# Another order for the first block of a fused state-space convolution and gated MLP: which pieces of two spectra PE takes first, and which engine evicts three of them

## The chip, the cores and the metric

One core of one Trainium2 chip. The metric is device time in microseconds of one execution, as the median of the runs; a profile is one more execution, taken by the hardware profiler, whose span runs from the first to the last instruction of the program. Engines are named as in the profile: PE (TensorE matmul) and PEld (its weight loads), DVE (VectorE), ACT (ScalarE), POOL (GpSimd), SP (SyncE, which here only issues transfers).

## The reference

Inputs are bf16: q, k, v of 2048 x 640, a convolution kernel ssm_k of 640 x 2048, and MLP weights of 640 x 1728, twice, and 1728 x 640. Cut to what is computed:

```
k_shift = sum over 4 taps of shifted k * shift_k
kv = k_shift * v
y  = irfft(rfft(kv, 4096) * rfft(ssm_k, 4096))[:2048] + kv * ssm_D
h  = q + layernorm(q) * y          # per channel, along the sequence
n  = layernorm(h)
out = h + (silu(n @ w_gate) * (n @ w_up)) @ w_down
```

## The kernel before

The sequence is cut into four blocks of 512 rows. For block j the kernel builds a spectrum G of its piece of ssm_k ("g") and a spectrum X of its kv, both as matmuls against a cosine and sine basis (WF, in two halves that are loaded apart: planes 0 and 2 use the first, planes 1 and 3 the second). It multiplies spectra on DVE (`mac`), comes back with an inverse transform (`inverse`, L698, basis WI), makes h and its normalised transpose, and runs the MLP (`ffn`, L769 and L845). The MLP of block j is woven into the transforms of block j + 1.

In block 0 every 640-wide row is treated as two halves of 320 columns, so that DVE can begin early. There are four planes (c0 to c3) and two halves: eight pieces for each spectrum.

- An X0 piece (L336 to L342): an even pair of 128x320 matmuls (rows 0 and 2), an eviction of the PSUM tile with a factor 2 (L319 on ACT, L322 on DVE), an odd pair (rows 1 and 3) that accumulates on the same tile and so must wait for that eviction, and a second eviction.
- A G0 piece (L350 to L355): four matmuls, an eviction, two matmuls with the weights "minus" (DVE makes these from WF, L912), an eviction. G0 needs block 0's g transposed: four sets of five transposes on PE (L411), each copied out by L413 on ACT or DVE.
- Block 1's g goes another way: ACT regroups it in one copy (L419), then four DMA transposes (L404, arena<-arena, one for each row r0 to r3) put it in place. Block 1's k comes in through four DMA transposes as well (L404, kT<-in_A_k_dram); these overwrite kT and so wait for the copy of its last column into the halo (L517, ACT). G1's pairs are two 128x320 matmuls, one for each half, with one eviction of 128x640.

There are four PSUM tiles "ps"; a tile is free again when its last eviction is done. Larger buffers lie in an arena of 22 units, given out in the order in which they came free.

`Plan.add` records every operation with its engine, its reads and writes. `Plan.run` then issues them in the order of a table written out by hand, ORDER; this sets the order on each engine, since each engine runs its own instructions in the order of issue and waits for what they depend on:

```
for i in ORDER:
    op = self.ops[max(i, ~i)]
    if i < 0:
        op.fn = op.other[2]
```

A negative entry ~n takes operation n's other engine: DVE in place of ACT for an eviction. Numbers that the change moves and that matter below: 92 to 115 are X0's matmuls and evictions (92/93 and 94/95 for c2's first half, 105 to 108 for c1's second half); 43 to 74 are G0's; 34 to 41 the transposes of block 0's g and their copies; 12, 13, 14, 15 the loads of g, WF's first half, WF's second half and ssm_D; 187 to 190 block 1's k transposes; 194 to 197 block 1's g transposes; 198 to 217 G1; 6 nine matmuls on the identity that PE runs while it waits; 75 and 80 block 0's taps (L490), 221 block 1's.

Of the kernel before, what the change touches and what calls it, by code (L numbers as in the profile page):

```python
# [44 lines left out]
UNITS = 22  # L45
SLOTS = {"row": 5, "sg": 3, "ps": 4, "sm": 10}
ORDER = (
# [943 lines left out]
```

## Time and profile before

| | us |
|---|---|
| median of 3 runs | 252.25 |
| the runs | 251.06, 252.25, 252.71 |
| the profiled execution | 251.19 |
| its span | 249.5 |
| PE busy | 237.7 |
| DVE busy | 197.6 |
| ACT busy | 174.0 |

How to read the rows: in a timeline, the first number is the start in microseconds from the span's start, the second the duration (of the whole group where "xN" stands at the end), then engine, line, operation, tiles written and read, shapes. "[1.03 <-DMA ...]" is the engine's idle time just before and what ended it; "issue" means that nothing that the profile shows was waited for. SPq is SP's instruction that issues a transfer. In rows that end in "KB, 5.8" or "x1, 5.8" the last number is the time from issue to landing.

### The profile page before, as it was taken

The page shows a single profiled execution, that of the slowest core. Times are in us where ns is not written, and L with a number is a line of the kernel's source. Part 1 is how long each engine was busy: PE and PEld are TensorE (multiplying, and loading weights), DVE is VectorE, ACT ScalarE, POOL GpSimd, SP SyncE. Part 2 cuts the span into 40 slices and gives each one's busy share as a digit, 9 for nine tenths or more (in the row PEclk, how much of TensorE's full clock was granted, in tenths as well). Part 3 has the DMA queues.
Part 4 walks back from the last instruction along what each step waited for, and adds up shares of the span by engine and source line. Part 5 has one row for each costly group of instructions (what it writes and reads, how often), then busy time and mean ns, then how long its engine had stood idle before and what let it go on. Part 6 is the DMA issues. An engine that isn't in the chain of part 4 may idle for free.

```text
span 249.5 us, 5148 instructions
## 1 busy us (share of the span) xinstructions
PE 237.7 (95%) x2125; PEld 152.5 (61%) x2125; DVE 197.6 (79%) x250; ACT 174.0 (70%) x300; POOL 52.4 (21%) x53
## 2 busy tenths in 40 slices
PE   3899988999999999999999999999999999999994
PEld 3467655888857766544466676454456785464662
DVE  2779998999999999999999899999999542131222
ACT  2399998999999977969598699984532865325100
POOL 0002002531230313124400503353702110000030
PEclk9999999999999999999999999999999999999999
DMA  6999899287998566690725569789592200000052
GB/s 204 353 264 144 229 342 355 65 208 114 143 297 283 167 99 130 109 206 6 119 43 133 105 94 216 132 155 162 97 206 29 26 0 3 0 0 3 0 79 79
DMA packets 37283, 33.66 MB, mean 135 GB/s; under 512 B 22470, under 2 KB 32076, under 8 KB 37260
## 3 DMA queue, kind: packets, MB, share of 16 engines
q1 hardware_dynamic: 32028, 22.03, 34.0%
q0 software_dynamic: 5232, 11.31, 25.4%
q8 instruction: 16, 0.26, 0.4%
q14 instruction: 7, 0.06, 0.1%
HBM read 16.29 MB, written 4.59 MB: 84 GB/s over the span
## 4 chain that ended last, share of the span: by engine, by line
PE 75%; ACT 9%; DMA 6%; DVE 6%; issue 2%; SPq 1%; DVEq 0%; ACTq 0%
PE ps L769 36%; PE ps L845 23%; PE ps L329 7%; PE ps L698 5%; ACT arena L319 4%; DMA arena<-in_A_ssm_k_dram 4%; DMA arena<-arena 3%; PE ps L490 2%; DVE arena L542 2%; PE ps L833 1%; PE ps L411 1%; ACT arena L419 1%; DVE tT L787 1%; ACT sg L783 1%; ACT row L722 1%
## 5 line engine op out<-in xcount | busy, mean ns | idle before, releaser
L769 PE MATMUL ps<-arena,wgu 128*128 128x512 bf16 (+1 forms) x680 | 118.2, 329 | 0.4 <-ACT arena L413 0.2
L769 PEld LDWEIGHTS <-wgu 128*128 128x128 bf16 x680 | 66.2, 98 | 45.0 <-issue 1.1
L845 PE MATMUL ps<-wd,tT 128*128 128x320 bf16 x416 | 59.1, 299 | 0.0
L845 PEld LDWEIGHTS <-tT 128*128 128x128 bf16 x416 | 39.8, 98 | 17.2 <-issue 1.6
L542 DVE TENSOR_TENSOR arena<-arena 128x2560 bf16<-128x2560 bf16 x30 | 43.9, 1486 | 0.2
L783 ACT ACTIVATE sg<-ps 128x1024 bf16<-128x1024 f32 (+1 forms) x28 | 27.1, 971 | 22.2 <-PE ps L769 22.0
L329 PE MATMUL ps<-arena,WF 128*128 128x320 bf16 x176 | 29.8, 299 | 1.7 <-ACT arena L319 0.9
L785 ACT CAST sg<-ps 128x1024 bf16<-128x1024 f32 (+1 forms) x24 | 23.6, 982 | 8.5 <-PE ps L769 3.6
L610 POOL TENSOR_TENSOR sm<-sm,neghalf 128x4 f32<-128x4 f32 (+1 forms) x10 | 17.9, 1793 | 42.9 <-DVE sm L646 42.6
L243 POOL DMA_DIRECT2D arena<-arena x11 | 13.4, 1218 | 60.7 <-DVE arena L542 27.6
L319 ACT CAST arena<-ps 128x640 bf16<-128x640 f32 (+1 forms) x47 | 24.8, 594 | 1.3 <-PE ps L329 1.0
L787 DVE TENSOR_TENSOR tT<-sg,sg 128x1024 bf16<-128x1024 bf16 (+1 forms) x24 | 15.9, 664 | 11.0 <-ACT sg L785 11.0
L329 PEld LDWEIGHTS <-WF 128*128 128x128 bf16 x176 | 17.1, 97 | 11.1 <-issue 2.7
L545 DVE TENSOR_TENSOR arena<-arena 128x2560 bf16<-128x2560 bf16 x14 | 20.8, 1488 | 0.2
L606 ACT ACTIVATE junk<-arena 128x640 bf16<-128x640 bf16 x28 | 20.6, 745 | 0.4 <-DVE arena L709 0.4
L319 ACT ACTIVATE arena<-ps 128x640 bf16<-128x640 f32 (+1 forms) x32 | 19.8, 654 | 0.8 <-PE ps L329 0.8
L698 PE MATMUL ps<-arena,WI 128*128 128x320 bf16 x96 | 15.8, 299 | 1.0 <-issue 0.8
L709 DVE SCALAR_TENSOR_TENSOR arena<-arena,sm,ps 128x640 bf16<-128x640 bf16 x16 | 13.7, 877 | 3.2 <-ACT ps L707 3.1
L850 ACT ACTIVATE row<-ps,sm 128x640 bf16<-128x640 f32 x12 | 9.5, 791 | 8.6 <-PE ps L845 8.1
L852 POOL DMA_DIRECT2D out_dram<-row x12 | 11.7, 1151 | 14.6 <-ACT row L850 14.6
L707 ACT ACTIVATE ps<-ps,sm 128x640 f32<-128x640 f32 x16 | 11.9, 767 | 3.4 <-PE ps L698 3.3
L698 PEld LDWEIGHTS <-WI 128*128 128x128 bf16 x96 | 9.0, 97 | 5.6 <-issue 1.8
(91 smaller groups left out, 236.8 us busy)
## 6 DMA issues: line engine op xcount, KB each, us to landing
arena<-arena POOLq DMA_DIRECT2D x11, 640.0 KB, 6.2
arena<-in_A_v_dram SPq DMA_DIRECT2D x4, 640.0 KB, 5.1
arena<-in_A_q_dram SPq DMA_DIRECT2D x4, 640.0 KB, 4.5
out_dram<-row POOLq DMA_DIRECT2D x13, 160.0 KB, 4.2
arena<-in_A_ssm_k_dram SPq DMA_DIRECT2D x3, 640.0 KB, 8.8
wd<-in_B_w_down_dram SPq DMA_DIRECT2D x2, 800.0 KB, 7.1
out_dram<-arena POOLq DMA_DIRECT2D x2, 640.0 KB, 5.9
wgu<-in_B_w_gate_dram SPq DMA_DIRECT2D x1, 800.0 KB, 5.9
```

The lines of the kernel that those rows point to most:

```text
L319: (lambda: nc.scalar.activation(dst(), src(), ACT.Copy, scale=2.0)) if twice else (lambda: nc.scalar.copy(dst(), src())),
L329: nc.tensor.matmul(ap(ps)[:, h, 0:NH], w, ap(src)[:, r, h * NH:(h + 1) * NH], start=(first and i == 0), stop=(last and i == len(rs) - 1), ...
L542: dve(1402, lambda: v.tensor_mul(to(), X.part(xs), H.part(hs)), [X.at(xs), H.at(hs)], [at])
L545: added(1402 * n - 69 * (n - 1), lambda: v.tensor_add(to(), to(), b()), to, b, [what], at, n)
L606: act(725, lambda r=r: nc.scalar.activation(waste(), ap(x)[:, r, :], ACT.Square, scale=D ** -0.5, accum_out=sm(s, MSQ, (r,))), [(x, r)], [ ...
L610: nc.gpsimd.tensor_tensor(sm(s, RSTD, rs), sm(s, VAR, rs), ap(neghalf)[:, 0:len(rs)], op=ALU.pow)
L698: nc.tensor.matmul(ap(ps)[:, w, 0:NH], m, src[:, w * NH:(w + 1) * NH], start=(i == 0), stop=(i == len(terms) - 1))
L769: nc.tensor.matmul(split(ap(ps), n)[:, i, :], w(k), ap(hT)[:, k, lo:lo + n], start=(k == 0), stop=(k == KT - 1))
L783: act(905 if wide_ else 490, lambda: nc.scalar.activation(of(sg), of(*gate), ACT.Silu), [(gate[0], gate[1] + i) for i in range(m)] + (psu ...
L785: op = plan.add("act", 905 if wide_ else 490, lambda: nc.scalar.copy(of(co), of(*up)), psu + [sg], [co] + tt, ("dve", 1135 if wide_ else 6 ...
L787: op.rest = dve(602 if wide_ else 336, lambda: nc.vector.tensor_mul(to(), of(sg), of(co)), [sg, co], tt)
L845: nc.tensor.matmul(ap(ps[hf])[:, hf, 0:NH], ap(tT)[:, c * BLK + at:c * BLK + at + P], ap(wd)[:, c, hf * NH:(hf + 1) * NH], start=False, st ...
```

## The change

The first 160 entries of ORDER hold the same operations in another order; from the 161st on the table is the same. Three X0 evictions (93, 95 and 108) go from ACT to DVE, one G0 eviction (54) goes from DVE to ACT; of the four copies of block 0's transposed g, DVE has 35 and 37 in place of 37, 39 and 41. WF's second half (14) is issued before block 0's g (12).

```
--- before.py
+++ after.py
@@ -45,13 +45,13 @@
 ORDER = (
     0, 1, 2, 3, 16, 18, -20, 5, 4, 8, 17, 26, 13, 186, 9, 20, 22, 7, 10, 11, -22, 24, -26, 23, 75, 76, 77, 78, 79,
-    6, 193, 80, 81, 82, 30, 92, 93, 15, 12, 38, 83, 34, -40, 14, 36, 32, 35, 94, 27, -38, 95, 96, 97, 42, 28, 40,
...
+    0, 1, 2, 3, 16, 18, -20, 5, 4, 8, 17, 26, 13, 186, 9, 20, 22, 7, 10, 11, -22, 24, -26, 23, 75, 14, 76, 77, 78,
+    79, 6, 80, 81, 193, 82, 92, -94, 109, 30, 32, 110, 12, 105, 106, 88, 89, 94, -96, 111, 15, 83, 112, 107, -109,
...
```

On ACT, behind the regrouping of block 1's g (the row L419). WF_88 is the basis, ps0 to ps3 the four PSUM tiles, kT_93 block 0's transposed k; L413 with 128x640 is a copy of block 0's transposed g. Before:

```order
L419 COPY arena_86<-arena_86 128x2560
L319 ACTIVATE arena_86<-ps2_74 128x320
L517 COPY kT_93<-kT_93 128x20
L413 COPY arena_86<-ps3_75 128x640
L319 CAST arena_86<-ps2_74 128x320
L319 ACTIVATE arena_86<-ps0_72 128x320
L319 ACTIVATE arena_86<-ps1_73 128x320
L319 ACTIVATE arena_86<-ps2_74 128x320
```

And now:

```order
L419 COPY arena_86<-arena_86 128x2560
L319 ACTIVATE arena_86<-ps0_72 128x320
L319 ACTIVATE arena_86<-ps3_75 128x320
L319 ACTIVATE arena_86<-ps1_73 128x320
L517 COPY kT_93<-kT_93 128x20
L319 CAST arena_86<-ps0_72 128x320
L319 CAST arena_86<-ps1_73 128x320
L413 COPY arena_86<-ps0_72 128x640
L319 ACTIVATE arena_86<-ps1_73 128x320
L413 COPY arena_86<-ps2_74 128x640
```

Three X0 evictions stand between the regrouping and the halo copy L517, where one stood, and the first copy of block 0's g on ACT comes after five evictions instead of one.

On SP, from the load of block 0's g (L289, in_A_ssm_k_dram; L903 is WF, L904 ssm_D, L301 x, L909 WI). Before:

```order
L289 DMA arena_86<-in_A_ssm_k_dram 128x5x512
L903 DMA WF_88<-const_wf 128x1024
L301 DMA arena_86<-in_A_q_dram 128x2560
L909 DMA WI_89<-const_wi 128x1024 x2
L404 DMA_TRANSPOSE arena_86<-arena_86 128x5x128
L301 DMA arena_86<-in_A_q_dram 128x2560
L404 DMA_TRANSPOSE arena_86<-arena_86 128x5x128 x2
L404 DMA_TRANSPOSE kT_93<-in_A_k_dram 128x5x128 x2
L404 DMA_TRANSPOSE arena_86<-arena_86 128x5x128
L404 DMA_TRANSPOSE kT_93<-in_A_k_dram 128x5x128 x2
```

And now:

```order
L903 DMA WF_88<-const_wf 128x1024
L289 DMA arena_86<-in_A_ssm_k_dram 128x5x512
L904 DMA arena_86<-in_A_ssm_D_dram 1x640
L301 DMA arena_86<-in_A_q_dram 128x2560
L909 DMA WI_89<-const_wi 128x1024 x2
L404 DMA_TRANSPOSE kT_93<-in_A_k_dram 128x5x128
L404 DMA_TRANSPOSE arena_86<-arena_86 128x5x128 x2
L404 DMA_TRANSPOSE kT_93<-in_A_k_dram 128x5x128
L404 DMA_TRANSPOSE arena_86<-arena_86 128x5x128
L301 DMA arena_86<-in_A_q_dram 128x2560
L404 DMA_TRANSPOSE kT_93<-in_A_k_dram 128x5x128
L404 DMA_TRANSPOSE arena_86<-arena_86 128x5x128
```

WF's second half has moved ahead of g. The transposes of block 1's k and g now alternate, a k transpose comes first, and block 1's x (the second L301) stands sixth among them instead of second. In both, the four rows of g are taken in the order r0, r1, r2, r3 before and r1, r0, r3, r2 now.

On DVE, behind the last product of block 0's kv (the row L513; L322 is an X0 eviction, L429 adds ssm_D to the first row of g). Before:

```order
L513 TENSOR_TENSOR arena_86<-ps1_73,arena_86 128x2x4x32
L912 TENSOR_SCALAR arena_86<-WF_88 128x4x128
L413 COPY arena_86<-ps0_72 128x640
L912 TENSOR_SCALAR arena_86<-WF_88 128x4x128
L413 COPY arena_86<-ps1_73 128x640
L429 TENSOR_TENSOR arena_86<-arena_86 1x640
L413 COPY arena_86<-ps3_75 128x640
```

And now:

```order
L513 TENSOR_TENSOR arena_86<-ps1_73,arena_86 128x2x4x32
L322 TENSOR_SCALAR arena_86<-ps2_74 128x320
L912 TENSOR_SCALAR arena_86<-WF_88 128x4x128 x2
L322 CAST arena_86<-ps2_74 128x320
L322 CAST arena_86<-ps3_75 128x320
L413 COPY arena_86<-ps2_74 128x640
L429 TENSOR_TENSOR arena_86<-arena_86 1x640
L413 COPY arena_86<-ps3_75 128x640
```

Three X0 evictions stand in front of the copies of g, which are two instead of three. On PE, seven X0 pairs, even and odd ones of c2 and c1, now stand between X0's first pair and the first transposes of block 0's g (L411), where none stood; the rest of X0 comes next, then G0's pieces almost in one run, with G1's first pairs near their end. Before, X0's and G0's pieces alternated.

11 rows, old and new, of the table ORDER are left out of this document.

## The prediction

> **What bounds the kernel now.** I read the page first: which engine has no room.
>
> ```profile
> PE 237.7 (95%) x2125; PEld 152.5 (61%) x2125; DVE 197.6 (79%) x250; ACT 174.0 (70%) x300; POOL 52.4 (21%) x53
> ```
>
> PE is busy for 237.7 of 249.5 us. Next comes the busy time by stretch, to see where the other 11.8 us lie; the columns are length, then PE, PEld, DVE, ACT and POOL, clock, DMA share, GB/s.
>
> ```profile
> 11.35:14.88 3.53, 2.50 (x27) 1.65 (x27) 2.18 (x7) 3.53 (x6) 0.00 (x0) 1.00 0.95 361
> 14.88:26.50 11.62, 11.62 (x86) 8.19 (x84) 11.38 (x25) 11.18 (x32) 1.73 (x2) 1.00 1.00 165
> 26.50:36.45 9.95, 9.78 (x197) 6.55 (x195) 9.88 (x15) 9.95 (x22) 0.00 (x0) 1.00 0.99 305
> 36.45:44.00 7.55, 5.33 (x40) 3.41 (x41) 6.62 (x13) 6.37 (x13) 1.88 (x1) 1.00 1.08 354
> 44.00:80.00 36.00, 35.41 (x302) 28.73 (x301) 34.94 (x41) 35.23 (x59) 10.44 (x8) 1.00 0.75 178
> ...
> 44.00:246.00 202.00, 201.41 (x1608) 127.70 (x1606) 161.79 (x179) 140.35 (x229) 48.26 (x44) 1.00 0.53 107
> ```
>
> From 44 to 246 us PE is busy for 201.41 of 202.00, and between 14.88 and 36.45 PE, DVE, ACT and the DMA engines are all full. So whatever the change does at the front reaches the end as a shift of everything behind it. The question is only when the first 160 places hand over. The timeline at both ends of that stretch, PE and DVE:
>
> ```profile
> 11.35 0.43 PE L329 MATMUL ps<-arena,WF 128*128 128x320 bf16 x2 [0.18 <-DVE arena L513]
> 12.81 1.03 PE L411 MATMUL ps<-ident,arena 128*128 128x128 bf16 x15 [1.03 <-DMA arena<-in_A_ssm_k_dram]
> 14.88 3.42 PE L329 MATMUL ps<-arena,WF 128*128 128x320 bf16 x24
> ...
> 28.89 0.70 PE L698 MATMUL ps<-arena,WI 128*128 128x320 bf16 x4 [0.15 <-ACT arena L319]
> 30.07 1.19 PE L490 MATMUL ps<-diag,kT 32*128 32x128 bf16 x112
> 31.19 0.72 PE L698 MATMUL ps<-arena,WI 128*128 128x320 bf16 x4
> 37.28 2.08 PE L698 MATMUL ps<-arena,WI 128*128 128x320 bf16 x14 [0.83 <-issue]
> ...
> 8.81 3.28 DVE L513 TENSOR_TENSOR arena<-ps,arena 128x512 bf16<-128x512 f32 x6 [1.52 <-PE ps L490]
> 14.13 0.29 DVE L912 TENSOR_SCALAR arena<-WF 128x512 bf16<-128x512 bf16 x1 [0.32 <-DMA WF<-const_wf]
> 21.16 0.48 DVE L322 CAST arena<-ps 128x320 bf16<-128x320 f32 x1
> 21.56 0.28 DVE L912 TENSOR_SCALAR arena<-WI 128x512 bf16<-128x512 bf16 x1
> 30.32 0.82 DVE L594 TENSOR_TENSOR arena<-arena 128x1280 bf16<-128x1280 bf16 x1
> ```
>
> PE's wait of 1.03 us for block 0's g (landed 12.8) is the one big hole in the stretch. At the hand-over all engines tie: block 1's taps start at 30.07, the inverse at 31.19, when L594 ends (30.32 + 0.82 = 31.14). ScalarE's rows show the third party:
>
> ```profile
> 10.91 2.51 ACT L419 COPY arena<-arena 128x2560 bf16<-128x2560 bf16 x1 [4.09 <-DMA arena<-in_A_ssm_k_dram]
> 13.31 0.46 ACT L319 ACTIVATE arena<-ps 128x320 bf16<-128x320 f32 x1
> 13.64 0.29 ACT L517 COPY kT<-kT 128x20 bf16<-128x20 bf16 x1
> 13.75 0.72 ACT L413 COPY arena<-ps 128x640 bf16<-128x640 bf16 x1
> 14.34 0.46 ACT L319 CAST arena<-ps 128x320 bf16<-128x320 f32 x1
> 16.63 1.45 ACT L319 CAST arena<-ps 128x320 bf16<-128x320 f32 x4
> 28.07 1.97 ACT L319 CAST arena<-ps 128x640 bf16<-128x640 f32 x3
> 29.81 0.84 ACT L606 ACTIVATE junk<-arena 128x640 bf16<-128x640 bf16 x1
> ```
>
> ACT is held by the 2.51 us regrouping of block 1's g until 13.31, then evicts to 29.81. The taps at 30.07 start when its last eviction (28.07 + 1.97 = 30.04) frees their PSUM tile.
>
> **The change, part by part.** Prices per instruction, from the rows above: a 320-column matmul (3.42 - 0.30)/23 = 0.136, so a pair 0.27 and four 0.54; five transposes (1.03 - 0.22)/14 x 5 = 0.29; an ACT eviction of 320 columns every (1.45 - 0.48)/3 = 0.32, done after 0.46; of 640 columns every (1.97 - 0.77)/2 = 0.60; an L413 copy on ACT 14.34 - 13.75 = 0.59; a DVE eviction every 21.56 - 21.16 = 0.40, done after 0.48.
>
> *Front.* Now PE has seven more X0 pairs ahead of the g transposes. I stepped them: the first at 11.35; its neighbour in the other half needs the whole kv (8.81 + 3.28 = 12.09), so 12.14; the two c1 pairs follow to 12.95 if WF's second half is there; then one odd pair whose first eviction DVE now takes, to 13.22. The next odd pair needs ACT, which comes only at 13.31, so 13.31 + 0.46 + 0.05 = 13.82; the last odd pairs follow ACT's pitch and end at 14.73. In place of one hole of 1.19 us (11.62 to 12.81) stand two, 0.52 and 0.59. PE has sent 16 matmuls, 2.2 us of work, by 14.73; before it had sent six and twenty transposes, 2.0. Gain here: 0.2 at most. Both DMAs have room: WF's half and g together moved 10.9 to 14.1 before, so the half should land by 12.3 (11.6 if it moves at 361 GB/s, 0.26 MB in 0.7 us), needed 12.41; g by 14.1, needed 14.73.
>
> *ACT.* Before: 31 evictions of 320, 8 of 640, one L413 and L517 (13.75 - 13.64 = 0.11): 9.9 + 4.8 + 0.6 + 0.1 = 15.4 us in the 16.50 from 13.31 to 29.81, so 1.1 idle. The change takes three X0 evictions off, gives one G0 eviction back, and swaps one g copy for two: 29 and 2, 15.3 us. Nearly nothing is saved; what counts is idling. A G0 piece costs PE 0.54 + 0.27 = 0.82 and ACT two evictions, 0.64; an X0 piece costs PE 0.54 and ACT 0.64; a G1 pair PE 0.27 and ACT 0.60. Before, X0 and G0 alternate and even out. Now X0 comes first (PE waits for ACT, 14 to 18 us), then six G0 pieces in a row (ACT waits 0.18 in each, 1.1 in all, 18 to 24 us), then G1 (PE waits again). With two waits for PE at the front (0.25, 0.23) and 0.2 at the tail, ACT idles 1.7 to 1.8: its last G1 eviction ends 0.4 to 0.6 later. I take 0.5.
>
> *DVE.* Three evictions more, one eviction and one g copy less: + 0.4. Its first hole fills, but it waits for the odd pairs: stepping gives the statistics 0.8 later and L594's end at about 31.5, not 31.14. That hides behind ACT's 0.5.
>
> *SP.* The moved transposes are SP's issues; their rows, and single landings:
>
> ```profile
> 13.45 1.29 SPq L404 DMA_TRANSPOSE arena<-arena  x1
> 14.80 0.57 SPq L301 DMA_DIRECT2D arena<-in_A_q_dram  x1
> 15.41 2.63 SPq L404 DMA_TRANSPOSE arena<-arena  x2
> 18.22 3.82 SPq L404 DMA_TRANSPOSE kT<-in_A_k_dram  x2
> 22.09 1.27 SPq L404 DMA_TRANSPOSE arena<-arena  x1
> 23.47 2.53 SPq L404 DMA_TRANSPOSE kT<-in_A_k_dram  x2
> 28.77 0.33 SPq L296 DMA_DIRECT2D arena<-in_A_v_dram  x1
> ...
> arena<-arena SPq DMA_TRANSPOSE x1, 5.8
> arena<-arena SPq DMA_TRANSPOSE x1, 2.8
> kT<-in_A_k_dram SPq DMA_TRANSPOSE x1, 3.1
> ```
>
> The first issue is now a k transpose. It must wait for the kT halo copy (L517), which stands behind three evictions on ACT: 13.31 + 3 x 0.32 + 0.29 = 14.6 instead of 13.45. G1's row 2 was third; now six transposes and x's load stand ahead of it. At 1.27 each it issues at 14.6 + 7.6 + 0.57 = 22.8 and, 2.8 later, lands at 25.6; at the old mean, (26.0 - 13.45 - 0.57)/8 = 1.50, at 24.2, and 5.8 later at 30.0. I take 27.2, nearer the low end because x's load, which stood ahead of the 5.8, then overlapped other loads. By the stepping PE asks for it at 26.5, when ACT has evicted row 0's pair, and six G1 and inverse steps stand behind it on PE. So 0.7 late, of which 0.3 disappears in waits PE has there for ACT anyway: + 0.4 (0 to 3). POOL's order is the same. SP's later row (v, 28.77) already waits for a G1 tile, so weight loads move with PE, no further.
>
> The Trainium skill, page "DMA: Bandwidth & Descriptors", section "Latency and other measured facts", gives DMA transposes 261 GB/s, which I estimate at 0.63 us for 160 KB. By it row 2 lands at issue pace, 25.6, and this term is 0, the sum 0.5. The trace disagrees: 165 GB/s at a DMA share of 1.00 from 14.88 to 26.50.
>
> *Sum.* 0.5 + 0.4 = 0.9 us later at the taps, and the same at the end. The profiled execution took 251.19 (span 249.5 and 1.69 around it), so 252.1. It lies 1.06 below the median of the runs shown; the mean of it and the three runs is 251.8, so I forecast **252.7 us**.
>
> **The rivals.**
> - *Transposes late* (slower). If SP keeps 1.50 to 1.6 per transpose, row 2 lands at 28.5 to 30, or block 1's last k transpose (now issued about 1 us later, + 3.1 to 5) comes after 30.6, and taps, inverse and ACT wait. It decides from a landing after 26.8, then one for one: + 2 to + 3.4, 253.8 to 255.2, say 254.5. For: 3.82 for two. Against: 1.27 in the later rows. Chance 0.17.
> - *ACT keeps full* (faster). If PE runs ahead and ACT loses its 1.7 us idle, the hand-over is bounded by 13.31 + 15.3 = 28.6, 1.2 early; the two new holes at PE's front take back 0.5 of it, so 0.7 early, 251.1. For: PE's 1.03 us hole is gone. Against: G0 alone is heavier on PE than on ACT. Chance 0.20.
> - *WF's half lands no sooner* (the change does not do what it says). At 14.1 the c1 pairs wait 1.7 us, of which about 0.7 hides behind ACT: 1.0 more than the forecast, 253.7. Against: landings followed issue order (10.9, 12.8, 14.1). Chance 0.08.
> - *The pause at 36.45 goes or grows.* PE stops 0.83 us with nothing to wait for ("issue"). The page's queues:
>
> ```profile
> q8 instruction: 16, 0.26, 0.4%
> ```
>
> Sixteen packets of 16 KB for PE's 4250 matmuls and weight loads, one per 266, say that a block of its code may have come late through full DMA queues (share 0.99 to 1.08). The order there is unchanged, so it should stay; without it 251.9. Chance 0.08. The Trainium skill, page "Runtime: NRT & Kernel Launch", section "Instruction fetch mechanics", calls such a block's cost "mostly hidden"; by it the pause is something else and cannot vanish. No run shows yet which holds.
>
> **How the numbers follow.** The forecast has 0.47. Its own range is 0.3 to 1.5 later and 0.6 of scatter between runs: 251.5 to 253.9. To leave out no more than 2 in 10 it reaches down to the fast rival and up to most of the late transposes: **251.0 to 254.7**. A measurement of this kernel tells about 1% (2.5 us) from no change: below 249.3 only if the fast rival meets a vanished pause, 0.02; above 254.3 to 254.8 in under half of the late-transpose case, 0.08; within 1% 0.90.
>
> **What would show it.** Right: a PE wait near 13.2 for ACT instead of 12.8 for DMA; short ACT waits for PE between 18 and 24 us; a PE wait near 26.5 for a transpose; taps at 30.6 to 31.5; the 0.83 us pause kept. Wrong: taps at or before 30.07, or ACT without idle between 18 and 24; a time under 251 or over 255.

## The result and the profile after

The changed kernel takes 254.7 us (median of 20 runs, 253.38 to 258.66) beside 252.13 of the kernel before (20 runs, 250.39 to 254.79): 1.16% slower, ratio 1.0116 with a 95% interval of 1.0092 to 1.0139. Measured a second time among the experiments it stood at 1.0125 [1.0093, 1.0157]. The forecast was 252.7, with a chance of 0.08 for slower by over 1%. The direction was right and the size was not: 2.6 us were lost where 0.9 were forecast, and the median lies on the upper end of the range. The ratios leave out executions more than 1.5% above the fastest of their kernel, the medians none.

The profiled execution took 255.35 us, its span 253.7. It lies 4.2 us above the profiled execution of before (251.19), further than the medians do: that one was a short one of its kernel, and this one has the half clock described below, which only half of the runs have. The page's first row, and the same stretches as before (length, then busy PE, PEld, DVE, ACT and POOL, clock, DMA share, GB/s):

```profile
PE 239.6 (94%) x2125; PEld 153.4 (60%) x2125; DVE 198.4 (78%) x251; ACT 174.6 (69%) x299; POOL 52.0 (20%) x53
```

```profile
11.35:14.88 3.53, 3.00 (x49) 2.08 (x42) 2.83 (x8) 3.45 (x7) 0.00 (x0) 1.00 0.89 337
14.88:26.50 11.62, 11.12 (x88) 7.61 (x86) 11.34 (x25) 11.18 (x30) 1.82 (x2) 1.00 0.86 146
26.50:36.45 9.95, 7.10 (x143) 4.65 (x144) 7.42 (x10) 5.85 (x13) 0.00 (x0) 0.83 0.70 172
```

Up to 26.5 nothing is lost. From 26.5 to 36.45 all three engines have holes at once (before, PE was busy for 9.78, DVE 9.88, ACT 9.95), and the granted clock, 1.00 everywhere before, is 0.83. TensorE's rows show where; in brackets the idle time before the group and what ended it:

```profile
11.79 0.43 PE L329 MATMUL ps<-arena,WF 128*128 128x320 bf16 x2 [0.16 <-DVE arena L513]
12.59 2.17 PE L329 MATMUL ps<-arena,WF 128*128 128x320 bf16 x14 [0.36 <-DVE arena L513]
14.60 1.00 PE L411 MATMUL ps<-ident,arena 128*128 128x128 bf16 x15
...
25.71 0.43 PE L329 MATMUL ps<-arena,WF 128*128 128x320 bf16 x2
29.35 2.11 PE L329 MATMUL ps<-arena,WF 128*128 128x320 bf16 x8 [3.21 <-DMA arena<-arena]
31.25 1.27 PE L698 MATMUL ps<-arena,WI 128*128 128x320 bf16 x4
...
34.66 1.18 PE L490 MATMUL ps<-diag,kT 32*128 32x128 bf16 x112
```

The 1.03 us wait for block 0's g is gone. In its place stands one of 3.21 us: the group at 29.35 begins with G1's row 2, and it waits for that row's transpose. The four matmuls at 31.25 take 1.27 us, where four took 0.70 before. Block 1's taps start at 34.66 instead of 30.07. SyncE's queue, and the landing of row 2 (the issue at 23.43; the last number is us from issue to landing):

```profile
14.47 1.30 SPq L404 DMA_TRANSPOSE kT<-in_A_k_dram  x1
15.82 2.59 SPq L404 DMA_TRANSPOSE arena<-arena  x2
18.52 1.67 SPq L404 DMA_TRANSPOSE kT<-in_A_k_dram  x1
20.24 1.28 SPq L404 DMA_TRANSPOSE arena<-arena  x1
21.56 0.58 SPq L301 DMA_DIRECT2D arena<-in_A_q_dram  x1
22.18 1.20 SPq L404 DMA_TRANSPOSE kT<-in_A_k_dram  x1
23.43 1.28 SPq L404 DMA_TRANSPOSE arena<-arena  x1
```

```profile
arena<-arena SPq DMA_TRANSPOSE x1, 5.9
```

23.43 + 5.9 = 29.3: the matmul starts as the row lands. Behind the hole the clock is halved. The clock in short stretches, the third number from the right:

```profile
29.10:29.40 0.30, 0.05 (x1) 0.06 (x2) 0.30 (x1) 0.00 (x0) 0.00 (x0) 1.00 1.03 279
29.40:29.70 0.30, 0.30 (x3) 0.20 (x4) 0.30 (x2) 0.00 (x0) 0.00 (x0) 0.82 1.06 303
29.70:30.00 0.30, 0.30 (x3) 0.18 (x2) 0.30 (x1) 0.11 (x1) 0.00 (x0) 0.50 0.99 354
...
32.70:33.00 0.30, 0.30 (x3) 0.18 (x2) 0.30 (x2) 0.00 (x0) 0.00 (x0) 0.50 0.00 0
33.00:33.30 0.30, 0.30 (x4) 0.19 (x3) 0.30 (x1) 0.00 (x0) 0.00 (x0) 0.99 0.00 0
```

It is 0.50 from 29.6 to 33.0, 3.4 us in which PE is always busy: 1.7 us of its work. ScalarE and VectorE stand for 2.70 and 2.13 us between 26.5 and 36.45; their waits name the same chain:

```profile
29.89 0.69 ACT L319 CAST arena<-ps 128x640 bf16<-128x640 f32 x1 [2.70 <-PE ps L329]
```

```profile
32.41 0.49 DVE L379 TENSOR_TENSOR arena<-arena 128x640 bf16<-128x640 bf16 x1 [2.13 <-ACT arena L319]
```

Behind the hand-over the two kernels are alike: from the taps to the end of the span it is 219.4 us before (249.5 - 30.07) and 219.0 after. In all 14 profiles of this study that remainder lies between 218.7 and 219.7. So the time is the start of block 1's taps, T, and some 219.2 + 1.7 us, and the experiments can be read by T.

### The profile page after: what moved, and what is told of

Same layout as the page of the kernel before. It is cut to its first block, busy times and chain, and to the rows that moved or that the text cites. A ratio compares the mean times of both kernels' runs of the same rounds, so it can differ in the third digit from the quotient of the medians.

```text
span 253.7 us, 5143 instructions
## 1 busy us (share of the span) xinstructions
PE 239.6 (94%) x2125; PEld 153.4 (60%) x2125; DVE 198.4 (78%) x251; ACT 174.6 (69%) x299; POOL 52.0 (20%) x53
## 4 chain that ended last, share of the span: by engine, by line
PE 76%; DVE 7%; DMA 7%; ACT 6%; SPq 2%; issue 1%; ACTq 0%; DVEq 0%
PE ps L769 36%; PE ps L845 23%; PE ps L329 7%; PE ps L698 6%; DMA arena<-arena 5%; PE ps L490 2%; DVE arena L542 2%; DMA arena<-in_A_k_dram 2%; ACT arena L319 1%; PE ps L411 1%; DVE arena L513 1%; PE ps L833 1%; SPq L404 1%; ACT arena L419 1%; DVE tT L787 1%
## 5 line engine op out<-in xcount | busy, mean ns | idle before, releaser
L329 PE MATMUL ps<-arena,WF 128*128 128x320 bf16 x176 | 31.2, 305 | 5.3 <-DMA arena<-arena 3.2
L610 POOL TENSOR_TENSOR sm<-sm,neghalf 128x4 f32<-128x4 f32 (+1 forms) x10 | 19.2, 1916 | 47.6 <-DVE sm L646 47.3
```

Of the source, the lines that this page charges most:

```text
L329: nc.tensor.matmul(ap(ps)[:, h, 0:NH], w, ap(src)[:, r, h * NH:(h + 1) * NH], start=(first and i == 0), stop=(last and i == len(rs) - 1), ...
L610: nc.gpsimd.tensor_tensor(sm(s, RSTD, rs), sm(s, VAR, rs), ap(neghalf)[:, 0:len(rs)], op=ALU.pow)
```

## The experiments

My theory on seeing this was that the place of G1's row 2 in SyncE's queue made the loss, and that the half clock was its consequence. The rivals were ScalarE's idling behind the grouped G0 pieces, VectorE's three evictions, and the order of the front. In the order, 187 to 190 are the transposes of block 1's k (r0 to r3), 194 to 197 those of its g (r0 to r3), 192 is the load of its x, 200 the matmul pair that wants row 2, and a minus sign turns an eviction to the other engine.

### Row 2 put forward: two kernels

```diff
-    124, 195, 207, 208, 126, 194, 63, 64, 190, 197, 69, 70, 198, 199, 130, 127, 192, 65, 66, 128, 189, 196, 212,
+    124, 195, 207, 208, 126, 194, 63, 64, 196, 190, 69, 70, 198, 199, 130, 127, 192, 65, 66, 128, 197, 189, 212,
```

> The changed kernel, with four entries of its order exchanged on SyncE's queue and nothing else: G1's row 2 is the fourth transpose instead of the seventh, row 3 the sixth, and k's r3, r2 and r0 come behind. In the changed kernel row 2 was issued at 23.43 us, landed at 29.3, and TensorE stood for it for 3.21 us, after which its clock was granted 0.50 for 3 us. If the late landing is what the change costs: row 2 is issued near 19 and lands by 24, the hole of 3.2 us and the half clock go, block 1's taps start near 30.5 instead of 34.7, and the time is 252.3 (251.6 to 253.0), that of the kernel before. If ScalarE's idling behind the grouped G0 pieces is the cost (the 0.5 of the prediction, more than it said): the hole goes to another wait, and the time stays at 254.2 to 255. If row 3, now sixth, comes late in its turn: 253 to 254, with a wait for a DMA at row 3's matmul.

The second kernel has the same order and takes 188 from its place at the head of the queue:

```diff
-    125, 188, 46, 59,
...
-    63, 64, 196, 190, 69,
+    125, 46, 59,
...
+    63, 64, 196, 188, 190, 69,
```

> As the kernel with row 2 fourth, and k's r1 behind G1's rows 1, 0 and 2 too, so that SyncE's first transpose does not wait for the kT halo copy on ScalarE (13.45 us instead of 14.5). If the queue's order is the whole loss: 252.0, up to 0.3 below the one with row 2 fourth, since what PE asks for was there in that one too. If the wait for the halo copy mattered by itself (all transposes 1.1 us earlier): 0.5 to 1 lower, 251.5. If k's last transposes now come late: a wait at block 1's taps, 253 to 254.

Measured: 1.0038 [1.0012, 1.0064] and 1.0051 [1.0028, 1.0074] against the kernel before (252.45 and 252.58 us beside 251.51). More than half of the loss, up to two thirds, goes with the exchange of a few entries on one queue; the engines' order is untouched. TensorE in the first:

```profile
26.98 0.75 PE L329 MATMUL ps<-arena,WF 128*128 128x320 bf16 x4 [0.18 <-ACT arena L319]
28.80 0.72 PE L329 MATMUL ps<-arena,WF 128*128 128x320 bf16 x4 [1.07 <-DMA arena<-arena]
29.36 0.71 PE L698 MATMUL ps<-arena,WI 128*128 128x320 bf16 x4
...
31.90 1.18 PE L490 MATMUL ps<-diag,kT 32*128 32x128 bf16 x112
```

Row 2 is there in time, and now row 3, behind x's load, is 1.07 us late: it was issued at 22.83 and landed 5.9 us later. That is the third outcome in the expectation, though it cost less time than I gave it. In the second kernel the queue starts earlier, since its first transpose doesn't wait for the halo copy:

```profile
13.93 3.92 SPq L404 DMA_TRANSPOSE arena<-arena  x3
18.03 2.83 SPq L404 DMA_TRANSPOSE kT<-in_A_k_dram  x2
20.90 0.58 SPq L301 DMA_DIRECT2D arena<-in_A_q_dram  x1
21.52 1.21 SPq L404 DMA_TRANSPOSE arena<-arena  x1
```

```profile
27.86 0.70 PE L329 MATMUL ps<-arena,WF 128*128 128x320 bf16 x4 [0.18 <-ACT arena L319]
28.44 0.70 PE L698 MATMUL ps<-arena,WI 128*128 128x320 bf16 x4
...
30.98 1.18 PE L490 MATMUL ps<-diag,kT 32*128 32x128 bf16 x112
```

No wait for a DMA is left, the clock stays at 1.00 there, and what PE waits for is ScalarE. (This kernel is called "rows first" below.) T is 30.98, 19.08 us behind PE's first X0 product (11.90), against 18.72 before: 0.36 later. By the runs' times it stands between 0.3 and 0.7% above the kernel before, not level with it, as I had expected; and it is no faster than the kernel with row 2 fourth, although its T is 0.9 earlier in the profiles.

### The same mistake made in the kernel before

```diff
-    71, 31, 72, 196, 200, 201, 187, 126, 63, 117, 127, 64, 189, 73, 74, 61,
+    71, 31, 72, 187, 189, 190, 188, 196, 200, 201, 126, 63, 117, 127, 64, 73, 74, 61,
```

> The kernel before, with its order of work kept and G1's row 2 put behind all four k transposes on SyncE (eighth thing instead of fourth). If a late row 2 is the loss, the kernel before gets it too: issued near 22.5, landing at 26 to 29, while TensorE asks for it near 24; a wait for a DMA of 2 to 4.5 us at that row's matmuls, a lower clock behind it, and 254.5 to 257. If the loss was in the other order of the engines' work: the wait falls into TensorE's waits for ScalarE, and the time stays at 252.1 to 252.6.

Measured: 1.0094 [1.0059, 1.0129], 253.8 us. So four k transposes put ahead of row 2 on SyncE's queue, with the engines' order untouched, make the kernel before nearly as slow as the change did, though it stays under the 254.5 that I expected at least. The profile shows the wait, though shorter than expected, and a clock of 1.00 behind it:

```profile
24.68 1.25 PE L329 MATMUL ps<-arena,WF 128*128 128x320 bf16 x8
26.84 0.99 PE L329 MATMUL ps<-arena,WF 128*128 128x320 bf16 x6 [0.91 <-DMA arena<-arena]
```

Row 2 was issued at 24.1 and took only 2.7 us to land here, with four k transposes between it and x's load. The wait of 0.91 explains the sign; the 1.5 to 3.2 us of the interval are more than this one execution shows.

### The half clock: idle matmuls in the hole

```diff
+        filled = len(plan.ops) == 200
+
         def mm():
+            for _ in range(26 if filled else 0):
+                nc.tensor.matmul(ap(ps)[:, 1, NH:512], ap(WF)[:, 0, 0, 0, :], ap(WF)[:, 1].rearrange("p r s q -> p (r s q)")[:, 0:192],
+                                 start=True, stop=True, skip_group_check=True)
             for i, r in enumerate(rs):
```

> The changed kernel, with 26 matmuls of 192 columns that compute nothing used (constants into unused columns of a PSUM tile) right in front of the row-2 matmul for which TensorE waits; about 26 x 0.082 = 2.1 us of work, so that 1.1 of the 3.2 us hole are left; the landing is not changed. If the half clock behind the hole (0.50 for 3 us) is a consequence of TensorE standing: the clock stays at 1.0 there, the work behind the hole takes 1.5 us less, and the time is 253.2 (252.9 to 253.7). If the clock falls for another reason (the memory traffic, the time since the start): still 0.50 at 30 to 33 us, and 254.7 as the changed kernel, or more.

Measured: 1.0102 [1.0070, 1.0134], 253.99 us, above the 252.9 to 253.7 that I expected. The clock stayed at 1.00 and the eight matmuls behind took 1.25 us instead of 2.11, but the time was not told apart from that of the changed kernel. 26 of them were too many: row 2 was there before they ended. So the next kernel had 14, beside the changed kernel itself.

> As the changed kernel with 26 idle matmuls in front of row 2, with 14 of them (1.15 us): enough to cut a hole of 3.2 us to 2.1, and less in the way where row 2 lands sooner. If the half clock is a consequence of how long TensorE stands (a hole of 1.95 left it at 1.00 in the kernel with k first, 2.83 and 3.21 halved it): no half clock at 30 to 33 us, and 0.5 to 1.4 us less than the changed kernel beside it, 253.3 to 254.2 where that gives 254.7. If the clock does not depend on the hole: the time of the changed kernel, or up to 1 more.

> The changed kernel once more, beside the one with 14 idle matmuls on the same chip: 1.1 to 1.3% above the kernel before; in a second profile row 2's landing (29.3 us in the first) and TensorE's hole (3.21) show how far they scatter: under a hole of about 2.4 us there should be no half clock.

Measured: 1.0071 [1.0041, 1.0102] (253.27 us) with the 14, 1.0125 [1.0093, 1.0157] (254.68 us) without: 1.4 us. With the 14:

```profile
26.84 1.31 PE L329 MATMUL ps<-WF 128*128 128x192 bf16 x14 [0.18 <-ACT arena L319]
29.36 1.25 PE L334 MATMUL ps<-arena,WF 128*128 128x320 bf16 x8 [1.21 <-DMA arena<-arena]
```

The row lands at the same moment as in the first profile of the changed kernel (29.36 and 29.35). PE does work of no use and loses nothing by it, and T is 33.11 instead of 34.66: the difference of 1.55 is the clock alone. A second profile of the changed kernel, an execution of 254.24 us, the fastest of its six, has the wait without the half clock:

```profile
29.83 1.26 PE L329 MATMUL ps<-arena,WF 128*128 128x320 bf16 x8 [2.28 <-DMA arena<-arena]
```

Row 2 landed at 29.3, 29.8 and 29.3 in the three profiles, from issues at 23.43, 24.71 and 24.57. So the landing is not a fixed time behind the issue; what sets it no run shows. What scatters is PE's start (11.66 to 13.09), and with it the hole: 3.21, 2.28, and 1.21 behind the idle matmuls.

How often the half clock comes can be read from the mean granted clock, which is on record for every execution: 3.4 us at half speed make it 0.993 (1 - 3.4/2/253.7). Of the 20 runs of the changed kernel ten stand at 0.993 or less (median 255.3 us) and ten at 0.998 or more (254.0); of the six of the second measurement three (255.6) and three (254.3); of the 18 runs with idle matmuls none is under 0.997. So the idle matmuls keep the half clock away, and it costs about 1.3 us in the half of the runs that have it. It is not the whole of the 1.4 us between the two medians: the three runs of the second measurement without it still lie 1.0 us above 253.27. What that part is stays open.

### The parts of the change, one by one

With G1's rows put first, so that no late row hides the rest, the basis's second half went back behind g (32, VectorE's "minus" weights made from it, moves along):

```diff
-    75, 14, 76, 77, 78, 79, 6, 80, 81, 193, 82, 92, -94, 109, 30, 32, 110, 12, 105,
+    75, 76, 77, 78, 79, 6, 80, 81, 193, 82, 92, -94, 109, 30, 110, 12, 14, 105,
...
-    34, -36,
+    34, 32, -36,
```

> The kernel with G1's rows first on SyncE (which stood 0.5% [0.3, 0.7] above the kernel before) with the basis's second half loaded behind block 0's g again, as before; the engines' new order of work and the three evictions on VectorE are kept. The two c1 pairs in front of g's transposes then want the half that landed at 14.1 us in the kernel before. If the earlier half is what makes the new front possible: TensorE waits for a DMA near 13 for about 1 us, g's transposes end about 0.7 later, the hand-over to block 1 moves by 0.4 to 0.8, and the time is 0.2 to 0.3% above the kernel with rows first. If the half lands at the same time in either order (the rival of the prediction): no difference. If the moved half was itself the rest of the loss (it delays g): 0.2 to 0.4% below it, the time of the kernel before.

Measured: 1.0043 [1.0010, 1.0076], not told apart from the 1.0051 with the half in front. The wait is there, about half as long as expected:

```profile
13.60 0.43 PE L329 MATMUL ps<-arena,WF 128*128 128x320 bf16 x2 [0.58 <-DVE arena L513]
14.61 1.80 PE L329 MATMUL ps<-arena,WF 128*128 128x320 bf16 x12 [0.57 <-DMA WF<-const_wf]
```

So the half does land later when it is issued later, and the new front needs it early; what the new front is worth is too small to measure. Next, the three evictions back on ScalarE, again with the rows first:

```diff
-    92, -94, 109,
+    92, 93, 109,
...
-    94, -96, 111,
+    94, 95, 111,
...
-    107, -109,
+    107, 108,
```

> The kernel with G1's rows first on SyncE, with the three X0 evictions back on ScalarE. If ScalarE sets the hand-over (its last eviction ended at 30.78 there): 3 x 0.32 us more on it, less what it idles between its grouped evictions, so block 1's taps 0.4 to 0.9 later and the time 0.2 to 0.4% above the kernel with rows first. If VectorE sets it (its L594 ended at 32.03 there, 20.13 behind TensorE's first product against 19.79 before): 0.4 net off VectorE, and the time 0.1 to 0.3% below, that of the kernel before. Where the first eviction (TensorE waits for VectorE's) now stands behind the 2.5 us regrouping: a hole of 0.5 to 1 us more in TensorE's front.

Measured: 1.0035 [1.0008, 1.0063], the same again. In its profile PE waits 0.61 us for ScalarE at 14.05, the hole in PE's front that I had named, and T is 19.87 us behind PE's first product, against 19.08 with the evictions on VectorE: 0.8 us in the trace, and not seen in the times. And each of the two edits alone in the kernel before:

```diff
-    193, 80, 81, 82, 30, 92, 93, 15, 12, 38, 83, 34, -40, 14, 36,
+    193, 80, 81, 82, 30, 92, 93, 15, 14, 12, 38, 83, 34, -40, 36,
```

> The kernel before with the load of the basis's second half in front of block 0's g and nothing else changed. 0.26 MB at 361 GB/s put g 0.7 us later, and the first hole of TensorE (1.03 us, to 12.81) becomes about 1.7. ScalarE is held by the regrouping until 13.3 anyway, and its next copy comes 0.2 to 0.4 later than it would: 0.1 to 0.3% above the kernel before. If landings don't follow the order of issue (the prediction's rival that the half lands no sooner): no difference, the hole stays near 1.0.

```diff
-    30, 92, 93, 15,
+    30, 92, -94, 15,
...
-    27, -38, 95, 96,
+    27, -38, -96, 96,
...
-    107, 108, 113,
+    107, -109, 113,
```

> The kernel before with the three X0 evictions on VectorE and nothing else changed: ScalarE 3 x 0.32 = 1.0 us lighter, VectorE 3 x 0.40 = 1.2 heavier, of which the first fits in VectorE's hole of 1.0 at 12.3 to 13.3. If VectorE's L594 (31.14) ties the hand-over: it ends 0.8 later, block 1's inverse with it, 0.2 to 0.3% above the kernel before. If ScalarE is the bound and VectorE has room: taps up to 1.0 earlier, 0.2 to 0.4% below it.

Measured: 1.0042 [0.9999, 1.0085] and 1.0023 [0.9988, 1.0058]: no gain in either, and no sure loss by these ratios; the medians are 253.59 and 252.62 beside 251.66. The half alone has its twelve times in two groups, 251.30 to 252.50 and 254.67 to 256.08. All six of the upper group have a mean granted clock of 0.993 or less, all six of the lower 0.997 or more. Its profile (256.08 us) is of the upper one and shows a half clock again, this time in the front, behind a wait of 2.83 us where I had expected 1.7:

```profile
12.56 0.45 PE L329 MATMUL ps<-arena,WF 128*128 128x320 bf16 x2
15.84 1.79 PE L411 MATMUL ps<-ident,arena 128*128 128x128 bf16 x15 [2.83 <-DMA arena<-in_A_ssm_k_dram]
```

```profile
14.60:15.00 0.40, 0.00 (x0) 0.00 (x0) 0.00 (x0) 0.15 (x1) 0.00 (x0) 0.85 0.61 228
15.00:15.40 0.40, 0.00 (x0) 0.00 (x0) 0.00 (x0) 0.00 (x0) 0.00 (x0) 0.50 0.40 149
...
21.40:21.80 0.40, 0.40 (x3) 0.26 (x2) 0.37 (x3) 0.40 (x1) 0.00 (x0) 0.61 1.31 211
21.80:22.20 0.40, 0.40 (x5) 0.29 (x4) 0.40 (x2) 0.33 (x2) 0.00 (x0) 1.00 1.28 284
```

0.50 from 14.9 to 21.7. PE works from 15.84, so 5.9 us at half speed cost 2.9. I tried idle matmuls there too, 16 in the kernel with the half alone and 12 in the kernel before, in front of g's first transposes:

```diff
+        filled = len(plan.ops) == 38
+
         def tr():
+            for _ in range(12 if filled else 0):
+                nc.tensor.matmul(ap(pt)[:, 1, NH:512], ap(WF)[:, 0, 0, 0, :], ap(WF)[:, 0].rearrange("p r s q -> p (r s q)")[:, 0:192],
+                                 start=True, stop=True, skip_group_check=True)
             for c in range(KT):
```

> The kernel before with the basis's second half in front of g, and 16 idle matmuls of 192 columns (1.3 us, constants into unused columns) in front of the first transposes of block 0's g. Without them its times fell in two groups, 251.3 to 252.5 and 254.7 to 256.1, and the profile of one of the second showed a hole of 2.83 us there and a clock of 0.50 for the 6 us behind it. If the hole makes the half clock: the upper group goes, all times in 251.3 to 253. If the two groups have another cause: they stay.

> The kernel before with 12 idle matmuls of 192 columns (1.0 us) in front of the first transposes of block 0's g, where TensorE stood 1.03 us for a DMA; nothing else. If the executions of the kernel before above 253.4 us (5 of 35) are those in which that hole was long enough to halve the clock: none of them here, the median 0.1 to 0.3 below or equal. If they are something else: the same spread as before.

Measured: 1.0065 [1.0035, 1.0094], times from 251.74 to 254.84 without a gap, and 1.0031 [1.0001, 1.0060], from 251.02 to 254.16. The times missed both expectations, the clock did not: all 24 runs have a mean of 0.997 or more. The half clock is gone in the first, but its times did not fall into the lower group, and nothing was won in the second; what else makes runs of up to 254.84 at full clock stays open. The upper runs of the kernel before are half-clock runs too: in its three measurements beside these kernels, all ten runs above 253.4 us (of 86) have a mean clock of 0.993 or less. Which wait halved it there no profile shows; the wait for block 0's g is a candidate, 1.03 us in the profile of before and 1.95 in the kernel with k first, whose front is the same. No variant beat the kernel before.

## Why the prediction went wrong, step by step

**What bounds.** Right. Whatever moved T reached the end: 219.0 us behind it after, 219.4 before. The pause at 36.45 took 0.4 of the difference: it was 0.83 before and is 0.40 now. I had said that it stays, since the order there is unchanged; over the profiles it ranges from none (rows first) to 1.14 us (k first), so it is not a fixed cost, and no run settles what it is.

**Front.** Right in kind: the 1.03 us hole went, and smaller ones took its place, 0.36 for L513 where 0.52 was stepped. The wait for ScalarE near 13.2 was not there in this execution; it shows in others (0.26 at 14.02 with row 2 fourth). A gain of 0.2 at most is neither shown nor refuted: the runs with the parts undone tell differences of about 1 us.

**ACT.** Right in kind, and nearer 0.3 than 0.5 in size. Its six G0 pieces in a row show no bracketed waits, and by the busy sum ScalarE is as full as before (11.18 us in both). The idling hides inside the group:

```profile
18.17 6.23 ACT L319 CAST arena<-ps 128x320 bf16<-128x320 f32 x16
```

(6.23 - 0.46)/15 is 0.385 for one, against the pitch of 0.32: 1.0 us of idling in short steps that the view joins into one busy group, beside the 1.1 that the prediction has for these pieces. But the kernel before has such groups too:

```profile
18.33 2.71 ACT L319 CAST arena<-ps 128x320 bf16<-128x320 f32 x7
23.41 3.04 ACT L319 CAST arena<-ps 128x320 bf16<-128x320 f32 x8
```

Their pitch is 0.375 and 0.369, some 0.7 us of idling in all, so the grouping itself added about 0.3. Where nothing else is late, with rows first, T is 0.36 later behind PE's first product, beside the 0.5 of the sum. Its L594 ends 20.13 us behind that product (before 19.79), 0.34 later, beside the 0.36 stepped for VectorE. Times put the rest, with the queue mended, at 0.3 to 1.9 us. What of it is these terms and what is scatter of the front's start (PE's first product lay between 11.35 and 13.09 us in the 14 profiles, in no order that follows the kernel) stays open.

**SP.** This is the step that failed. Its issue time was nearly right, 23.43 against 22.8. But I took the landing at 27.2, 4.4 us behind the issue, "nearer the low end because x's load, which stood ahead of the 5.8, then overlapped other loads", and reasoned the 5.8 away. The runs say the opposite. Of g's transposes issued shortly behind x's load, row 2 before took 5.8 us, row 2 after 5.9, again 5.1 and 4.7, and the rows 3 of the two mended kernels 5.9 and 5.8; over all profiles the recorded ones took 4.7 to 6.9. With k transposes in between, row 3 before took 2.8, and with k first row 2 took 2.7 (with the half alone row 3 took 4.4); ahead of the load g's took 2.7 to 5.1. The load is the neighbour that all those of over 5.1 share; no run moved it alone, so that it is the cause is argued and not shown. The row of before that I needed was the one for the same neighbour, not a value between the two: 22.8 + 5.8 = 28.6. PE also was done with the work ahead of the row earlier than stepped, at 26.14 instead of 26.5, although its front began 0.44 later. So the row was 3.2 us late, not 0.7, and 2.3 in the second profile.

**One for one.** Also wrong, and left out of every case: a long wait can cost more than its length. The half clock behind it took 1.55 us in the profiles, and half of the runs have it. By the measured ratios, of the 1.25% go 0.54 with the idle matmuls (1.0125 to 1.0071) and 0.33 more with row 2 put forward (to 1.0038), and 0.38 remain: 1.4, 0.8 and 0.9 us. The first two are known to about 1 us either way, so the second is not told from none.

**The rivals.** The late transposes came true, at the time that was given for it (254.5), with a chance of 0.17 that was too small: the profile had two durations for such a row, and the larger was that behind x's load. The condition was not the one given: the six transposes ahead took 1.40 us each ((23.43 - 0.57 - 14.47)/6), not 1.50 to 1.6, and the long landing did it. That the time fits is partly luck, since the rival prices the wait one for one and has no half clock. ACT keeping full was wrong: it idles in its groups (0.385 a piece instead of 0.32), and T is no earlier behind PE's start in the mended kernels (20.35 and 19.08, before 18.72). WF's half did land sooner when put first.

**Transposition by its bandwidth.** The Trainium skill's 261 GB/s (page "DMA: Bandwidth & Descriptors", section "Latency and other measured facts") gave a row at issue pace and a term of 0. The trace disagrees: the landings read here took 2.7 to 6.9 us for 160 KB.

## What to carry to other kernels

When a step is moved on a queue, price it by the row whose neighbours on that queue are the new ones (here: shortly behind a large load, 4.7 to 6.9 us instead of 2.7 to 5.1), and compare with the moment at which its consumer asks, not with its old place. Keep the loads that nobody needs yet behind the transfers that TensorE will ask for. And a wait of TensorE of about 3 us can have a second price, the half clock behind it, which idle matmuls in the wait (14 here) can save where the wait itself can't be taken away. The mean granted clock of each run tells which runs paid it.

## What the runs showed of the hardware

The granted clock was halved for 3.4 us in the changed kernel (29.6 to 33.0) and for 6.8 us, twice that, in the kernel with the half alone (14.9 to 21.7). The mean clocks of the other runs lie where none (0.997 or more), one (0.991 to 0.993) or two (0.985 and 0.987) such stretches put them, so it seems to change in steps of one length. It fell 3.5 us after PE had stopped in the one case (26.14) and 1.9 us after in the other (13.01), so the steps don't start with the wait. Waits of 3.21 and 2.83 us halved it, waits of 2.28, 1.95 and 1.21 did not. If the same wait does so or not as it falls into the steps, that would make the two groups of times of one kernel; this is argued, since no two profiles show one wait with both outcomes. The Trainium skill, page "TensorE: Matmul & The Clock Gate", section "What's actually happening", has the rate halved after an idle window of about 3.4 us on a free-running count, and restored after a busy one: the traces agree on the length. If the clock falls where such a window ends, the window need not be idle throughout: PE had stood for only 1.9 us when it fell in the second case.
